# First batch's row fetches in 16 KB pieces, one table for both row parities, wider stand-in matmuls and two moved items

## The chip, the cores and the metric

The kernel runs on one core of a Trainium2 chip. The metric is the device time of one execution in microseconds (us). The engines are named as the profile names them: PE (TensorE, with its weight loads as PEld), DVE (VectorE), ACT (ScalarE), POOL (GpSimd) and SP (SyncE, which here only issues DMAs). All data are fp32.

## The reference

Eight batches of 3008 tokens by 256 channels go through a spectral filter along the token axis, and the result, as one list of 24064 tokens, goes through a two-layer block with SiLU:

```python
def _attn_ref(x, filt_r, filt_i):            # x: 8 x 3008 x 256
    X = np.fft.rfft(x, axis=1)
    Y = X * (filt_r + 1j * filt_i)[None, :, :]
    return np.fft.irfft(Y, n=x.shape[1], axis=1)

def _moe_ref(x, w_in, w_out):                # x: 24064 x 256, w_in: 256 x 2048, w_out: 2048 x 256
    h = x @ w_in
    return (h * (1.0 / (1.0 + np.exp(-h)))) @ w_out
```

## The kernel before

The transform of length 3008 is done as small matmuls: 3008 = 94 x 32, so a batch is 94 rows of 32 columns n. Stage 1 transforms along the rows (tiles `pa`, or `pf` in later batches), `forward` along the columns (`pb`), DVE multiplies with the filter, `inverse` goes back along the columns (`pc`), and stage 3 goes back along the rows (`pd`). Its results are copied into `y`, which feeds the two-layer block. [...]

The two-layer block is one long loop of 384 steps, 48 pairs of token groups by 8 slices of the hidden layer. Each step multiplies two slices of `w_in` (lines 1001 and 1047, tiles `px` and `pyz`) and projects the step before (line 1093, tile `acc`). From step 6 on the block products are done with seven matmuls in place of eight, by a Strassen-like scheme; `tokens` (line 978) makes the sums of token blocks that it needs (tile `ty`, three DVE instructions for one pair). The spectral work of the later batches is slipped into the steps at hand-written places: `put(step, round, piece)` appends a piece to `pending`, and `until` writes out what is due. Each engine works its own instructions in the order in which the program writes them.

The first batch comes before the loop and is written out by hand (lines 1338 to 1453). For it `inverse_first` gives, for each of six groups g, tiles `pc` that `rows_first` copies to SBUF and `store_half` (line 700) sends to `d2[0]` (columns 0 to 15) and later to `d2[1]` (columns 16 to 31). `fetch_rows` (line 723) brings `d2[0]` back with the summed axis on the partitions, in three pairs of DMAs on SP's queue, for rows 0 to 15, 16 to 31 and 32 to 47. The element order of a row in `d2` is (n, h, c): column n of 16, row parity h of 2, channel c of 256. A DMA of a pair takes one parity h: 16 rows of 16 pieces of 256 channels (1 KB each), onto partitions of the lower half (h = 0) or the upper half (h = 1) of the tile `us["t4"]`, which lies in the still unused weight tile `w_t`. The third pair waits for the stores of groups 4 and 5, the last of which is issued at line 700 by SP.

Stage 3 of group g (line 730) then multiplies four columns, `t4[rows, i, ...]`, with the table `wi_t` (at this time filled from `ws_tbl`: for each parity the 64 rows of that parity's partitions). `pd_g_0` holds parity 0, from the lower partitions, and `pd_g_1` parity 1. `evict_y` (line 757) copies them into `y`, in four runs of 47. Groups 0 to 3 make columns 0 to 15, that is pairs 0 to 2 of the loop, groups 4 to 7 the other half, with another load (`load_t4`). Groups 0 to 2 come before the loop, group 3 in step 1. For groups 0 to 2 ACT copies `pd_g_0` and DVE `pd_g_1`; for group 3 DVE copies `pd_3_0` and ACT `pd_3_1`.

Before the loop the eight PSUM banks go round by a counter, `early[0]` (line 354): each new tile takes the next of f, f, a0, a1, a2, a3, x, yz. `idle(n, operand, m)` (line 1324) is n matmuls of m columns that compute nothing that is used; it takes a bank of its own and so moves the counter by one. There are two: 26 of 36 columns at the start, before the first data are there (line 1341), and 2 of 96 columns ahead of stage 3 (line 1436).

The chain around that place is, in the order of the program:

```python
    out_of(3, 2, copy=act)
    gp.tensor_copy(out=gate, in_=part["us"]["t4"][:, 0, 0:1])
    ...
    idle(2, m=96)
    early[0] -= 1
    part["stage3"](0)
    out_of(3, 3, copy=act)
    early[0] += 2
    part["stage3"](1)
```

Here `out_of(3, q)` copies the four tiles `pa_3_q` that the second batch's stage 1 (line 425) has made just before; q = 0 and 1 go to DVE, 2 and 3 to ACT.

The second batch's pieces are placed by `plan` (line 827), relative to step 48: `multiply` (line 621) is two DVE instructions of 128x512 that read `pb` and the filter. The tokens of pair 2 are written by lines 1499 to 1501.

Of the kernel before, what the change touches and what calls it, by code (L numbers as in the profile page):

```python
# [46 lines left out]
FP32 = mybir.dt.float32  # L47
# [8 lines left out]
N1, N2 = 47, 64  # L56
# [218 lines left out]
def kernel(  # L275
# [10 lines left out]
    nc = tc.nc  # L286
    ctx.enter_context(tc.manual_schedule())

    wx_host, wq_host, wi_host, d_host, e_host = dft_tables()
# [1 line left out]
    wx3_dram = nc.inline_tensor(np.tile(wx_host.reshape(3, 32, 128).transpose(1, 0, 2), (4, 1, 1)).copy(), name="wx3_tbl")  # L291
    wq_dram = nc.inline_tensor(wq_host, name="wq_tbl")
    wi_dram = nc.inline_tensor(wi_host, name="wi_tbl")
    ws_host = np.zeros_like(wi_host)
    for k, (first, by) in enumerate(SPREAD):
        for h in range(2):
            ws_host[64 * h + first:64 * h + first + 15 * by + 1:by] = wi_host[64 * h + 16 * k:64 * h + 16 * k + 16]
    ws_dram = nc.inline_tensor(ws_host, name="ws_tbl")
    d_dram = nc.inline_tensor(d_host, name="d_tbl")
    e_dram = nc.inline_tensor(e_host, name="e_tbl")  # L300
# [9 lines left out]
    cpool = pool("consts", 1)  # L310
# [18 lines left out]

    wx_t = cpool.tile([96, 128], FP32)  # L330
    wq_t = cpool.tile([128, 4, 32], FP32)
    wi_t = cpool.tile([128, N1], FP32)
    wm_t = cpool.tile([128, 32], FP32)
    d_t = cpool.tile([128, NS, 2, 32], FP32)
    e_t = cpool.tile([128, NG, 2, 2, 64], FP32)
# [16 lines left out]
    y = {}  # L352
# [18 lines left out]
    def spectral(b):  # L371
# [3 lines left out]
        d2 = dpool.tile([2 * NS, 32, 2, C] if b else [2, 2 * NS, 16, 2, C], FP32, name=f"d2_{b}", tag="d2")  # L375
        xs, us, t2s, banks, prods, halves, t4s = {}, {}, {}, {}, {}, {}, {}
# [346 lines left out]
        def fetch_rows(a0, n, *queues):  # L723

            k, r0 = divmod(a0, 16)
            for h in range(2):
                queues[h].dma_start(out=us["t4"][64 * h:64 * h + 64].rearrange("(q r) n c -> q r n c", r=4)[r0:r0 + n, k],
                                in_=d2[0, a0:a0 + n, :, h, :])

        def stage3(g, home=None):  # L730

            half, n0 = divmod(4 * g, 16)
            ps = [bank(b, f"pd_{b}_{g}_{h}", home[h] if home else None)
                  .rearrange("p a c -> p (a c)")[:, 0:8 * N1]
                  .rearrange("p (a i n) -> p a i n", a=2, i=4) for h in range(2)]
            t4 = us["t4"][:, 4 * g:4 * g + 4] if g < 4 else t4s[g]
            for cb in range(2):
                for i in range(4):
                    for c0 in (0, 64):
                        for h in range(2):  # L740
                            rows = slice(64 * h, 64 * h + (64 if g < 4 else 2 * NS))
                            nc.tensor.matmul(  # L742
                                out=ps[h][c0:c0 + 64, cb, i, :],
                                lhsT=t4[rows, i, 2 * c0 + cb:2 * c0 + 128:2],
                                rhs=wi_t[rows, :], start=True, stop=True)
            if 3 < g < 6:
                load_t4(g + 2)
            if n0 == 0:
                y[b, half] = ypool.tile([128, 2, HALF], FP32, name=f"y_{b}_{half}", tag="y")
            if early[0] is None:  # L750
                us["pd", g] = ps
                return
            us["pd", g] = ps
            for h in range(2):
                evict_y(g, h, nc.vector.tensor_copy if h else nc.scalar.copy)

        def evict_y(g, h, copy=None):
            half, n0 = divmod(4 * g, 16)
            dst = y[b, half].rearrange("p a (n h r) -> p a h n r", n=16, h=2)
            copy = copy or (nc.scalar.copy if h else nc.vector.tensor_copy)  # L760
            copy(out=dst[:, :, h, n0:n0 + 4], in_=us["pd", g][h])

        def load_wide(k):
            t4s[k] = [t4pool.tile([128, 8, C // 2], FP32, name=f"t4_{b}_{k}_{cb}", tag="t4") for cb in range(2)]
# [56 lines left out]
    def put(step, rnd, piece, *args):  # L821

        pending.append((step + rnd / ROUNDS, len(pending), lambda: piece(*args)))
# [3 lines left out]
    def plan(b, part):  # L827

        at = STEPS * b

        if b > 1:
            put(at - {2: 80, 3: 120}.get(b, 128), 0, part["reverse_x"])
            early_fold = (-73, ((-68, 3), (-68, 5), (-65, 3), (-64, 3))), (-89, ((-82, 5), (-81, 3), (-81, 5), (-75, 5)))
            for f, step, load, places, ends in (
                    (0, -64, *early_fold[b > 2], ((1, 0), (1, 3))),
                    (1, -56, -63, ((-61, 5), (-60, 3), (-60, 5), (-59, 3)), ((1, 3), (2, 3))),
                    (2, -48, -55, ((-52, 3), (-52, 5), (-51, 5), (-50, 5)), ((1, 3), (2, 3)))):
                put(at + load, 4 if load == -89 else 0, part["load_fold"], f)
                for k, (fold_step, rnd) in enumerate(places):
                    put(at + fold_step, rnd, part["fold"], f, k)  # L840
                put(at + step, 7, part["stage1_fold"], f)
                put(at + step, 7, part["evict_fold"], f)
                for q, (after, rnd) in enumerate(ends):
                    put(at + step + after, rnd, part["pairs_fold"], f, q)
                joined.add(at + step)
                opened.add(at + step + 1)
            put(at - 47, 0, part["load_fold"], 3)
            for k, (step, rnd) in enumerate(((-45, 3), (-45, 5), (-44, 3), (-44, 5))):
                put(at + step, rnd, part["fold"], 3, k)
            early_out.add(at - 43)  # L850
            open_step(at - 43, (part["stage1_fold"], 3), (part["evict_fold"], 3))
            put(at - 43, 3, part["pairs_fold"], 3, 0)
            put(at - 43, 5, part["pairs_fold"], 3, 1)
            return plan_two(b, part)
        put(at - 38, 0, part["load_t2"], 0)
        put(at - 38, 0, part["load_t2"], 1)
        for g, places in enumerate((
                ((-36, 3), (-36, 5), (-35, 3), (-35, 5), (-34, 5)),
                ((-35, 6), (-34, 3), (-33, 3), (-33, 5), (-32, 1)),
                ((-32, 7), (-31, 0), (-31, 2), (-28, 5), (-27, 2)),  # L860
                ((-27, 3), (-27, 5), (-26, 5), (-25, 3), (-24, 3)),
                ((-24, 7), (-23, 0), (-23, 2), (-20, 2), (-20, 5)),
                ((-20, 3), (-19, 3), (-19, 5), (-18, 3), (-18, 5)))):
            pieces = (("forward", g), ("multiply", g, 0), ("multiply", g, 1), ("add", g, 0), ("add", g, 1))
            for (step, rnd), (piece, *args) in zip(places, pieces):
                if piece != "forward" or g in (1, 3, 5):
                    put(at + step, rnd, part[piece], *args)
        open_step(at - 36, *last_part[0](5), (part["forward"], 0))
        for g, step in ((0, -32), (2, -24), (4, -16)):
            put(at + step, 7, part["inverse"], g, 2)  # L870
            if g < 4:
                pending.append((at + step + 7 / ROUNDS, 10 ** 6 + 9, lambda g=g: part["forward"](g + 2, ACCS)))
                joined.add(at + step)
            put(at + step, 7, part["even"], g, 0, 2)
            put(at + step, 7, part["even"], g, 1, 2)
            put(at + step + 1, 5, part["rows"], g, 0, 2)
            put(at + step + 2, 3, part["rows"], g, 1, 2)
        plan_rest(b, part)
# [445 lines left out]
    def idle(n, operand=None, m=128):  # L1324

        ps = bank(0, "idle").rearrange("p a c -> p (a c)")
        rows = (wx_t if operand is None else operand)[:, 0:m]
        for _ in range(n):
            nc.tensor.matmul(out=ps[0:m, 0:m], lhsT=rows, rhs=rows, start=True, stop=True)
# [8 lines left out]
    wide_rows = d_t[0:96].rearrange("p s r n -> p (s r n)")[:, 0:256]  # L1338
    blank = w_t.rearrange("p j c w n -> p (j c w n)")[0:96, 6144:6272]
    v.memset(blank, 0.0)  # L1340
    idle(26, operand=blank, m=36)

    part, second = spectral(0), spectral(1)
    part["load_first"]()
# [5 lines left out]
    nc.sync.dma_start(out=f_all[:, :, 4:], in_=filt_b)  # L1350
    nc.sync.dma_start(out=d_t[:, 16:NS], in_=d_dram[:, 16:NS])
    nc.sync.dma_start(out=e_t[:, 2:NG], in_=e_dram[:, 2:NG])
    nc.sync.dma_start(out=wi_t, in_=ws_dram.ap())
    weights(0, 1)
    second["load_pair"](1)
    second["load_pair"](2)
# [76 lines left out]
            for i in range(2):  # L1433
                part["store_half"](g, i, 1, gp)
    halves_of(2, 3)
    idle(2, m=96)
    early[0] -= 1
    part["stage3"](0)
    out_of(3, 3, copy=act)
# [53 lines left out]
    per = len(PAIRS) * 2  # L1493


    combines = ((-2, 1), (6, 1), (11, 5), (22, 1), (26, 6), (38, 1))
    stores = (((10, 1), (10, 5)), ((19, 1), (23, 5)), ((31, 1), (31, 5)), ((35, 1), (35, 5)),
              ((43, 1), (43, 5)), ((50, 1), (51, 1)))
    for pair in range(len(pairs)):
        step, rnd = combines[pair % per] if pair > 2 else ((5, 2), (11, 1), (12, 1))[pair]  # L1500
        pending.append((pair // per * STEPS + step + rnd / ROUNDS, 98, lambda pair=pair: tokens(pair)))
        for chunk in range(2 if pair < len(pairs) - 1 else 0):
            step, rnd = stores[pair % per][chunk] if pair else (14, 1 + 4 * chunk)
            pending.append((pair // per * STEPS + step + rnd / ROUNDS, 99 + chunk,
                            lambda pair=pair, chunk=chunk: output(pair, chunk)))
# [65 lines left out]
```

## Time and profile before

| | |
|---|---|
| median of 3 executions | 2485.16 us (2485.12 to 2485.7) |
| the profiled execution | 2485.27 us |
| its span, first to last instruction | 2483.1 us |
| around the span | 2.2 us |
| PE busy | 2472.1 us, 16272 matmul records |
| DVE, ACT, POOL busy | 1748.4, 1087.1, 438.9 us |
| granted TensorE clock, mean | 1.000 |
| DMA | 170.68 MB, mean 69 GB/s |

The profile is of one execution. Its groups of instructions give busy time, mean duration and the idle time of the engine ahead of them, with what ended it. The timeline lists instructions in order of time, merged where they follow each other. The chain of waits follows the last instruction back through whatever released each step. One fp32 matmul of the program shows as two matmul records and two weight loads. Positions such as 48.8 us are counted from the start of the span.

### The profile page before, as it was taken

The numbers are of one execution on the slowest core, as the hardware profiler recorded it, in microseconds if no ns is written. First come the engines' busy times: TensorE is split into PE (matmuls) and PEld (weight loads), VectorE is DVE, ScalarE is ACT, GpSimd is POOL, SyncE is SP. The second block draws the span as 40 slices with busy tenths as digits, with TensorE's granted clock in tenths as the row PEclk, the third lists the DMA queues.
The fourth block names the chain that finished last, engine by engine and source line by source line (L and its number), as shares of the span: only waits on it lengthen the run. The fifth ranks groups of instructions, "written<-read, shape, count | busy, mean of one in ns | idle before, by whom it ended". The sixth has DMA issues, their size and how long they took to land.

```text
span 2483.1 us, 42315 instructions
## 1 busy us (share of the span) xinstructions
PE 2472.1 (100%) x16272; PEld 2124.9 (86%) x16272; DVE 1748.4 (70%) x3577; ACT 1087.1 (44%) x2986; POOL 438.9 (18%) x683
## 2 busy tenths in 40 slices
PE   9999999999999999999999999999999999999999
PEld 6888888888888888888888888889888888888988
DVE  7876777777777777786777767777777767655544
ACT  4534444444444444444444444444444444444443
POOL 4121112112221112211221112211221121101100
PEclk9999999999999999999999999999999999999999
DMA  8432225203242033320333114221142211200000
GB/s 327 148 98 77 74 63 117 63 14 93 61 109 61 25 78 81 96 54 26 88 83 89 49 29 108 60 69 43 51 98 47 56 51 32 59 22 9 17 10 17
DMA packets 139881, 170.68 MB, mean 69 GB/s; under 512 B 20972, under 2 KB 113484, under 8 KB 139148
## 3 DMA queue, kind: packets, MB, share of 16 engines
q1 hardware_dynamic: 116416, 121.74, 18.4%
q0 software_dynamic: 22272, 44.89, 6.9%
q8 instruction: 128, 2.10, 0.4%
q10 hardware_dynamic: 992, 1.36, 0.2%
q14 instruction: 73, 0.60, 0.1%
HBM read 96.06 MB, written 81.26 MB: 71 GB/s over the span
## 4 chain that ended last, share of the span: by engine, by line
PE 99%; DVE 0%; DMA 0%; POOL 0%; ACT 0%; issue 0%; SPq 0%; DVEq 0%
PE acc L1093 46%; PE px L1001 26%; PE pyz L1001 19%; PE pd L779 1%; PE pf L504 1%; PE pc L598 1%; PE pb L560 1%; PE pa L401 1%; PE pc L676 0%; PE px L1047 0%; PE pyz L1047 0%; PE pb L542 0%; PE pd L742 0%; PE pc L656 0%; DMA d<-w_t 0%; DMA w_t<-d 0%
## 5 line engine op out<-in xcount | busy, mean ns | idle before, releaser
L1093 PE MATMUL acc<-g,w_t 128*128 128x256 f32 (+1 forms) x5388 | 1513.1, 376 | 3.0 <-ACT o L792 2.5
L1093 PEld LDWEIGHTS acc<-g,w_t 128*128 128x128 f32 x5388 | 1019.8, 190 | 153.1 <-ACT o L792 15.3
L972 DVE TENSOR_TENSOR g<-pyz,abc 128x256 f32<-128x256 f32 (+1 forms) x1134 | 472.3, 416 | 468.2 <-ACT abc L1022 228.4
L972 DVE TENSOR_TENSOR g<-g 128x512 f32<-128x512 f32 (+1 forms) x1134 | 581.3, 513 | 193.8 <-ACT g L1005 180.8
L1001 PE MATMUL px<-ty,w_t 128*128 128x256 f32 (+1 forms) x2268 | 665.5, 375 | 0.0
L1005 ACT ACTIVATE g<-g 128x256 f32<-128x256 f32 (+1 forms) x1134 | 465.4, 410 | 231.9 <-DVE g L972 231.9
L972 POOL TENSOR_TENSOR s<-s 128x256 f32<-128x256 f32 (+1 forms) x331 | 254.3, 785 | 1436.4 <-DVE s L1121 981.8
L1001 PEld LDWEIGHTS px<-ty,w_t 128*128 128x128 f32 x2268 | 427.9, 190 | 52.1 <-issue 0.8
L1001 PE MATMUL pyz<-y,w_t 128*128 128x256 f32 (+1 forms) x1512 | 444.0, 375 | 1.1 <-DVE g L972 1.1
L1001 PEld LDWEIGHTS pyz<-y,w_t 128*128 128x128 f32 x1512 | 279.4, 189 | 42.3 <-DVE g L972 2.9
L1016 ACT COPY abc<-px 128x256 f32<-128x256 f32 (+1 forms) x378 | 139.1, 368 | 366.6 <-PE px L1001 366.6
L1005 ACT ACTIVATE g<-px 128x256 f32<-128x256 f32 (+1 forms) x378 | 143.5, 380 | 298.1 <-PE px L1001 298.0
L1022 ACT COPY abc<-px 128x256 f32<-128x256 f32 (+1 forms) x378 | 139.2, 368 | 307.3 <-PE px L1001 307.2
L1001 PE MATMUL px<-y,w_t 128*128 128x256 f32 (+1 forms) x756 | 223.5, 377 | 0.0
L1001 PE MATMUL pyz<-ty,w_t 128*128 128x256 f32 (+1 forms) x756 | 222.1, 376 | 0.0
L1001 PEld LDWEIGHTS px<-y,w_t 128*128 128x128 f32 x756 | 141.7, 189 | 21.1 <-DVE q L800 1.9
L1001 PEld LDWEIGHTS pyz<-ty,w_t 128*128 128x128 f32 x756 | 139.9, 190 | 20.2 <-DVE g L972 0.4
L1009 ACT COPY abc<-px 128x256 f32<-128x256 f32 (+1 forms) x378 | 133.0, 352 | 34.5 <-PE px L1001 34.5
L524 POOL DMA_DIRECT2D d<-tf x96 | 48.5, 505 | 212.9 <-DVE tf L454 212.9
L1121 ACT COPY s<-acc 128x512 f32<-128x512 f32 (+2 forms) x99 | 56.1, 566 | 49.0 <-issue 28.5
L619 POOL DMA_DIRECT2D d<-low x36 | 22.3, 618 | 292.5 <-DVE low L615 279.0
L494 DVE TENSOR_TENSOR uf<-x_all 120x512 f32<-120x512 f32 (+1 forms) x72 | 60.2, 864 | 0.3 <-issue 0.3
(134 smaller groups left out, 1390.2 us busy)
## 6 DMA issues: line engine op xcount, KB each, us to landing
t<-d SPq DMA_DIRECT2D x84, 256.0 KB
t<-d SPq DMA_DIRECT2D x224, 96.0 KB
out_dram<-s SPq DMA_DIRECT2D x64, 256.0 KB
d<-q POOLq DMA_DIRECT2D x48, 256.0 KB, 5.3
x_all<-in_x_dram SPq DMA_DIRECT2D x96, 96.0 KB
x_all<-xr SPq DMA_DIRECT2D x96, 96.0 KB
d<-tf POOLq DMA_DIRECT2D x96, 96.0 KB, 2.7
d<-tq POOLq DMA_DIRECT2D x96, 96.0 KB, 2.8
```

The costliest lines, as they stand in the source:

```text
L401: nc.tensor.matmul(out=ps[q], lhsT=wx3_t[rows, k], rhs=xs[j][rows, k], start=(k == 0), stop=(k == 2), skip_group_check=True)
L494: nc.vector.tensor_tensor(out=out, in0=in0, in1=in1, op=op)
L504: nc.tensor.matmul(out=ps[q][32 * k:32 * k + 32], lhsT=wq_t[rows, k], rhs=rhs[k][rows], start=True, stop=True)
L524: nc.gpsimd.dma_start(out=d1[par, :, grp, at:at + 4], in_=part[rows].rearrange("p q n c -> p (q n) c"))
L972: eng.tensor_tensor(out=out, in0=in0, in1=in1, op=op)
L1001: nc.tensor.matmul(out=out, lhsT=w_t[:, jp, c, 0], rhs=rhs, start=start, stop=True, skip_group_check=True)
L1005: nc.scalar.activation(out=g[:, k, 0:n], in_=g[:, k, 0:n] if src is None else src, func=AFT.Silu)
L1009: nc.scalar.copy(out=sums[:, 0, 0:n], in_=xo)
L1016: nc.scalar.copy(out=sums[:, 1, 0:n], in_=xo)
L1022: nc.scalar.copy(out=sums[:, 2, 0:n], in_=xo)
L1093: nc.tensor.matmul(out=acc[pair][i][:, h, 0:n], lhsT=w_t[:, jp, OUT_PLACE.get(c, c), 1], rhs=g[:, k, 0:n], start=i not in touched, stop=la ...
L1121: copy(out=dst, in_=src)
```

## The change

- `fetch_rows` splits a row by columns in place of parities: the first DMA of a pair takes columns 0 to 7, the second columns 8 to 15, both parities, so that each row is one run of 4096 elements (16 KB). The lower partitions then hold columns 0 to 7 and the upper ones 8 to 15, with the parities alternating along the free axis.
- The table gets a place for each parity on all partitions: `ws_t` [128, 2, 47] in place of `wi_t` [128, 47]; its load doubles from 188 to 376 bytes per partition. `wi_t` is its first half and is reloaded at step 5 as before.
- Stage 3 of groups 0 to 3 takes the table by `i % 2`, so `pd_g_0` now holds columns 2g and 2g + 1, both parities, and `pd_g_1` columns 8 + 2g and 9 + 2g. `evict_y` writes one run of 188 for these groups in place of four of 47; the layout of `y` is as before.
- The stand-ins at the start are 16 of 58 columns in place of 26 of 36. Those ahead of stage 3 are gone, while `early[0] -= 1` behind them stays.
- `multiply(0, 0)` of the second batch goes from step 12, round 5 to step 12, round 3, and the tokens of pair 2 from step 12, round 1 to step 12, round 0.

The number of PE instructions falls by 12 matmuls; on every other engine the number is the same.

```diff
-    ws_host = np.zeros_like(wi_host)
+    ws_host = np.zeros((2, 64, 2, N1), wi_host.dtype)
     for k, (first, by) in enumerate(SPREAD):
         for h in range(2):
-            ws_host[64 * h + first:64 * h + first + 15 * by + 1:by] = wi_host[64 * h + 16 * k:64 * h + 16 * k + 16]
+            ws_host[:, first:first + 15 * by + 1:by, h] = wi_host[64 * h + 16 * k:64 * h + 16 * k + 16]
+    ws_host = ws_host.reshape(128, 2 * N1)
...
-    wi_t = cpool.tile([128, N1], FP32)
+    ws_t = cpool.tile([128, 2, N1], FP32)
+    wi_t = ws_t[:, 0]
...
-                queues[h].dma_start(out=us["t4"][64 * h:64 * h + 64].rearrange("(q r) n c -> q r n c", r=4)[r0:r0 + n, k],
-                                in_=d2[0, a0:a0 + n, :, h, :])
+                queues[h].dma_start(out=us["t4"][64 * h:64 * h + 64].rearrange("(q r) n c -> q r (n c)", r=4)[r0:r0 + n, k],
+                                in_=d2[0, a0:a0 + n, 8 * h:8 * h + 8].rearrange("a n h c -> a (n h c)"))
...
-                                rhs=wi_t[rows, :], start=True, stop=True)
+                                rhs=ws_t[rows, i % 2 if g < 4 else 0], start=True, stop=True)
...
-            dst = y[b, half].rearrange("p a (n h r) -> p a h n r", n=16, h=2)
             copy = copy or (nc.scalar.copy if h else nc.vector.tensor_copy)
-            copy(out=dst[:, :, h, n0:n0 + 4], in_=us["pd", g][h])
+            if g < 4:
+                dst = y[b, half].rearrange("p a (k n r) -> p a k n r", k=2, r=N1)[:, :, h, n0:n0 + 4]
+            else:
+                dst = y[b, half].rearrange("p a (n h r) -> p a h n r", n=16, h=2)[:, :, h, n0:n0 + 4]
+            copy(out=dst, in_=us["pd", g][h])
...
-                ((-36, 3), (-36, 5), (-35, 3), (-35, 5), (-34, 5)),
+                ((-36, 3), (-36, 3), (-35, 3), (-35, 5), (-34, 5)),
...
-    idle(26, operand=blank, m=36)
+    idle(16, operand=blank, m=58)
...
-    nc.sync.dma_start(out=wi_t, in_=ws_dram.ap())
+    nc.sync.dma_start(out=ws_t.rearrange("p h n -> p (h n)"), in_=ws_dram.ap())
...
     halves_of(2, 3)
-    idle(2, m=96)
     early[0] -= 1
     part["stage3"](0)
...
-        step, rnd = combines[pair % per] if pair > 2 else ((5, 2), (11, 1), (12, 1))[pair]
+        step, rnd = combines[pair % per] if pair > 2 else ((5, 2), (11, 1), (12, 0))[pair]
```

## Prediction

> **What bounds the kernel.** I read the page first: whether one engine fills the span, and whether the chain that ended last leaves it.
>
> ```profile
> PE 2472.1 (100%) x16272; PEld 2124.9 (86%) x16272; DVE 1748.4 (70%) x3577; ACT 1087.1 (44%) x2986; POOL 438.9 (18%) x683
> ...
> PE 99%; DVE 0%; DMA 0%; POOL 0%; ACT 0%; issue 0%; SPq 0%; DVEq 0%
> ```
>
> PE is idle for 2483.1 - 2472.1 = 11 us in all. A change that leaves the matmuls alone can only win back idle PE time, and 0.2% of the time (5 us, about what a measurement of this kernel can tell from no change) is nearly half of that. So next I read what PE waited for (total, times, longest):
>
> ```profile
> PE acc L1093 <- ACT o L792: 2.5, 3, 0.8
> PE pd L742 <- DMA w_t<-d: 1.4, 2, 0.9
> PE pyz L1001 <- DVE g L972: 1.1, 1, 1.1
> ```
>
> The first row lies in later batches, out of reach of the diff. The second is stage 3 waiting for the row fetches, the third lies at 141 us, in step 13. The rest of the span is matmul behind matmul, so what is won at these two places stays won. PE's timeline at the first place (start, length):
>
> ```profile
> 47.68 0.58 PE L1329 MATMUL idle<-wx_t 96*96 96x96 f32 x4
> 48.82 0.29 PE L742 MATMUL pd<-wi_t,w_t 64*64 64x47 f32 x2 [0.56 <-DMA w_t<-d]
> 49.99 3.09 PE L742 MATMUL pd<-wi_t,w_t 64*64 64x47 f32 x190 [0.89 <-DMA w_t<-d]
> 53.01 1.13 PE L1047 MATMUL px<-y,w_t 128*128 128x256 f32 x4
> ```
>
> Useful work ends at 47.75 (line 425's last matmul) and goes on in earnest at 49.99: 2.24 us, of which the stand-ins fill 0.58. The chain of waits tells why:
>
> ```profile
> 40.22 4.83 DMA d<-w_t
> ...
> 45.75 4.11 DMA w_t<-d
> 49.99 3.09 PE pd L742 x190
> ```
>
> The last store of group 5 is issued at 40.22 and lands at 45.05; only then SP issues the third fetch pair, whose second half lands at 49.86.
>
> **The fetches.** Bytes, number of DMAs and queue stay; the pieces change from 1 KB to 16 KB. By the trace's packet records a 1 KB packet takes 46 ns at the median, one of 8 KB 314 ns, one of 32 KB 1213 ns. Half of the last is 607 ns for 16 KB, against 16 x 46 = 736 ns, or some 850 ns at the 50 to 55 ns that crowded 1 KB packets take. All 16 engines work on a fetch (one row each), so a pair takes 1.2 us in place of 1.5 to 1.7: 0.3 to 0.5 us less. This counts twice: the first pair (issued at 37.76) lies ahead of the last stores in SP's queue, and the third is awaited itself. The other bound is the only packets of just this size, PE's instruction pages on the queue of kind "instruction": 1095 ns, by which a pair takes 2.2 us, 0.5 to 0.7 more. [...]
>
> The store has more to lose. By its semaphore records 15 of its 16 parts were confirmed by 43.64 and the last at 45.05; the stores beside it show the same straggler (43.27, then 44.57; 43.45, then 44.79). At 42.03 an instruction page of PE begins that takes 1.44 us. Stores with nothing in the way took 2.0 to 2.7 us (37.21 to 39.18, 35.48 to 38.20). The change takes 10 matmuls, 40 records, out ahead of this point, so the page falls due 40 records later, about 2.3 us at the pace of line 425 (144 records in 8.4 us), near 44.3. The store then lands at 43.6 or sooner. The page now meets the third pair; it can cost the engine it sits on up to 1.1 us.
>
> ```profile
> 41.16 5.19 SPq L727 DMA_DIRECT2D w_t<-d  x4
> 46.40 1.54 SPq L1208 DMA_DIRECT2D raw<-in_moe_w_dram  x3
> ```
>
> The row of 5.19 holds two pairs and SP's wait for the store between them. SP issued the third pair at 45.19 and 45.75, and it landed 3.4 and 4.1 us later (48.57, 49.86). Issued at 43.7 and 44.3 it lands by 47.1 and 48.4 with nothing else gained, some 0.5 us sooner with the larger pieces. What SP has queued behind (weights, then line 447's stores) moves up with it, by about as much as PE, so the weights arrive no later relative to their use; the nearest, raw 3, lands at 53.27 for a use at 54.52.
>
> **The removed stand-ins.** They cost nothing where PE waits anyway. But `early[0] -= 1` stays, so the banks shift by one: `pd_0_0` moves from a0 to the first f, which holds `pa_3_2` until ACT has copied it. The instruction order shows the new wait: on ACT in place of PE. ACT's row for that copy starts at 47.78 and takes 0.58, so stage 3 cannot start before 48.36 + 0.1 = 48.46. Behind the waiting matmul the whole PE queue waits. This, and not the fetch, is late next. `pd_1_1` goes to bank x (free at 48.0, DVE) and `px` waits for its copy by DVE, which ends near 51.1; `pyz` of step 0 now needs `pd_2_0`'s copy by ACT, which ends near 52.0, for a start at 52.4. Both fit, with 0.4 us to spare. Step 2 now needs `pd_3_0`, copied by DVE from 62.21 to 62.76; its first matmul came at 64.78.
>
> So stage 3 starts at 48.46 in place of 49.99: **-1.5 us**. Cover gone (ACT or the page late by 1 us): -0.5.
>
> **The copies into y and the table.** Four copies on ACT of 478 ns, four on DVE of 550 ns, in longer runs: I take no change; one copy's 0.5 us is the bound either way, since only the last one of ACT is near the path. The table's load is 24 KB more at 13 us, for a use at 48 us: nothing.
>
> **The stand-ins at the start.** 52 records took 3.34 us from 1.08. With 58 columns, 32 records take between 32 x 60 ns = 1.9 (if the pace does not go by width) and 32 x 97 ns = 3.1 us (if it does). The first real matmul waits for a load that lands at 4.17. Nothing, if PE reaches full speed as before: line 401's groups come 0.85 us apart until 7.92 and 0.43 from 8.55 on. One group more at the slow pace costs 0.4 us, and an earlier switch gives at most 0.3, as the loads end that.
>
> **The two moved items.** DVE around step 12:
>
> ```profile
> 134.80 0.42 DVE L972 TENSOR_TENSOR g<-pyz,abc 128x256 f32<-128x256 f32 x1 [1.59 <-ACT abc L1009]
> 135.14 0.88 DVE L972 TENSOR_TENSOR g<-g 128x256 f32<-128x256 f32 x2
> 135.94 0.65 DVE L972 TENSOR_TENSOR ty<-y 128x480 f32<-128x480 f32 x1
> 136.62 0.85 DVE L972 TENSOR_TENSOR ty<-y,ty 128x240 f32<-128x240 f32 x2
> ...
> 139.05 0.68 DVE L635 TENSOR_TENSOR z<-pb,filt 128x512 f32<-128x512 f32 x1
> 139.65 0.68 DVE L635 TENSOR_TENSOR p<-pb,filt 128x512 f32<-128x512 f32 x1
> 140.25 0.42 DVE L972 TENSOR_TENSOR s<-acc,s 128x256 f32<-128x256 f32 x1
> 140.58 0.42 DVE L972 TENSOR_TENSOR g<-pyz,abc 128x256 f32<-128x256 f32 x1
> ```
>
> PE's stall at 141.05 is the last row: it frees the bank that step 13 writes. DVE was idle for 1.59 us ahead of 134.80. In the new order the three `ty` instructions (1.45 us) come first and fill that time, with no wait of their own in the program; `z` and `p` (1.20 us) take their place at 135.94. The next sum still waits for ACT's copy (136.94 + 0.38), so it and the four copies of `acc` keep their times up to 139.05; then come the `s` row and the last sum, at 139.38. No DMA is moved. PE could go on at 139.71 and now does at 139.87: **-1.2 us** (bounds 0 to -1.34).
>
> **Sum**, against the profiled execution's 2485.27 (0.1 over the median): -1.5 - 1.2 = -2.7, **2482.6 us**.
>
> **Rivals.** (a) *Fetches no sooner.* The straggler stays, or the page holds up the third pair: stage 3 starts near 49.9, and only step 12 gains: 2484.1. For it: the store's landing hangs on one page's place. [...] (b) *Step 12's stall stays or moves on*, because another wait ends last there: 2483.8. Against it: each predecessor's row is above. (c) *Slower: too few DMA engines take the 16 pieces.* The copy at line 460, 46 rows of 32 KB, ran two packets at a time for 28 us. On two engines a half takes 8 x 0.607 = 4.9 us, six halves 29, and stage 3 starts near 69: +18, 2503. On four it is near 54.8, 2489; from five engines up the kernel is still faster. Against it: the present fetch has the same 16 rows outermost, and 16 engines confirm it; line 460 has 2 outermost. [...]
>
> **Chances.** Forecast 0.6, (a) 0.2, (b) 0.1, (c) 0.05, the rest 0.05 either way. The range of 8 in 10 takes in (a) and (b), and below the forecast the early switch and step 12's bound: 2481.7 to 2484.7. Faster by over 0.2% 0.03, within 0.92, slower 0.05, by the stalls' sizes and (c).
>
> **What would show it.** 16 KB packets near 610 ns on SP's queue; the last store landing near 43.5; stage 3 starting near 48.5 behind ACT's copy of `pa`; no wait of PE for DVE near 139.9. Wrong if the fetch lands after 48.4, if `px` or `pyz` of steps 0 to 2 shows a wait, or if a wait for weights turns up in the first steps.

## The result, and the profile after

The changed kernel takes 2490.57 us (median of 22 executions, 2484.34 to 2492.88), the kernel before 2486.16 us (22 executions beside them, 2484.57 to 2487.77): a ratio of 1.0017, 95% interval 1.001 to 1.0023. The forecast was 2482.6 us, in a range up to 2484.7; the change made the kernel some 4.4 us slower, not 2.7 us faster. The profiled execution took 2490.95 us with a span of 2488.5 us, 5.4 more than before.

PE's busy time hardly changed, so the page's first lines tell little (before: 2472.1 us of 2483.1):

```profile
PE 2474.1 (99%) x16248; PEld 2124.1 (85%) x16248; DVE 1749.3 (70%) x3577; ACT 1088.7 (44%) x2986; POOL 439.0 (18%) x683
```

What PE waited for, in the changed kernel (total, times, longest):

```profile
PE pd L744 <- issue: 3.7, 1, 3.7
PE acc L1098 <- ACT o L797: 2.5, 3, 0.8
PE pc L678 <- issue: 1.2, 1, 1.2
PE idle L1334 <- DVE w_t L1345: 1.1, 1, 1.1
PE pd L744 <- ACT w_t L444: 0.7, 1, 0.7
```

(Line numbers have moved: 425 is now 427, 676 is 678, 742 is 744, 1047 is 1052.) Both rows that the prediction set out to remove are gone: no wait for DVE in step 13, and at stage 3 a wait for ACT's copy in place of the fetches, as forecast. In their place stand two rows released by "issue", time in which the engine waited for nothing that the profile shows. PE's timeline places the large one in the middle of stage 3 (start, length, idle time ahead):

```profile
49.41 2.01 PE L744 MATMUL pd<-ws_t,w_t 64*64 64x47 f32 x115 [0.67 <-ACT w_t L444]
55.08 2.37 PE L744 MATMUL pd<-ws_t,w_t 64*64 64x47 f32 x77 [3.67 <-issue]
57.38 2.07 PE L1052 MATMUL px<-y,w_t 128*128 128x256 f32 x4
59.25 1.91 PE L1052 MATMUL pyz<-y,w_t 128*128 128x256 f32 x4
60.96 1.36 PE L1052 MATMUL px<-y,w_t 128*128 128x256 f32 x4
62.16 1.03 PE L1052 MATMUL pyz<-y,w_t 128*128 128x256 f32 x4
```

Before, stage 3's burst was one row of 3.09 us, and the `px` and `pyz` groups behind it took 1.13 and 1.03 us. So there are two losses: 3.67 us of nothing, and then matmuls at nearly twice their length. The windows of the changed kernel say what the second is (us, busy times, then the granted clock PEclk, DMA share, GB/s):

```profile
48.00:51.40 3.40, 2.73 (x121) 1.95 (x116) 2.09 (x4) 1.58 (x4) 3.12 (x6) 1.00 0.87 271
51.40:55.10 3.70, 0.04 (x6) 0.02 (x3) 0.00 (x0) 0.27 (x1) 2.88 (x6) 0.96 0.97 334
55.10:61.60 6.50, 6.50 (x87) 5.60 (x87) 5.10 (x10) 1.73 (x5) 4.09 (x9) 0.50 0.84 274
61.60:68.00 6.40, 6.40 (x64) 5.42 (x66) 2.77 (x5) 3.96 (x8) 4.10 (x9) 1.00 0.84 292
```

The granted clock is 0.50 until 61.6. The trace's clock record has it from 54.80 for 6.83 us, twice 3.41, and 54.80 lies 14 times 3.41 us behind the moment at which full clock began (7.01). In the 3.41 us just ahead of it (51.39 to 54.80) PE was idle for 3.38 us. Less was enough elsewhere: with the old start stand-ins put back (the first experiment below) half clock also followed 3.41 us with 1.39 us of idle PE (47.79 to 51.20), while in the run with two weight loads moved it did not follow 3.41 us with 1.63 us of idle PE (50.13 to 53.54). So the runs show no amount of idle time at which the clock falls.

What "issue" stands for is seen by counting. I counted PE's records (matmuls, weight loads and semaphore waits) from the start of the program. PE stopped behind record 961 (the 1.15 us at 35.44, line 678) and behind record 1473, 512 later. The queue of kind "instruction" with 127 packets of 16 KB fits PE: its 16248 matmuls and as many weight loads, 32496 records, are 256 for each packet.

```profile
q8 instruction: 127, 2.08, 0.3%
```

So I take both stops to be at page boundaries, two pages apart, a page being one such packet. A page is named here by the record at its boundary, reckoned in steps of 256 from the two stops. When each page's packet started, from the packet records, with the PE record that was then running:

```
                         page for record 961   page for 1217     page for 1473      page for 1729
before                   30.50 (at 810)        34.98 (999)       42.03 (1188)       54.94 (1696)
changed                  34.10 (926)           38.68 (1040)      52.68 (1473)       58.56 (1634)
```

In the changed kernel the page that holds stage 3's second half starts at 52.68, 1.26 us after PE ran dry at 51.42, takes 1.03 us, and PE goes on 1.37 us after its end. Before, it had landed (43.47) nearly 8 us ahead of use. The 40 records of the ten start stand-ins are missing ahead of it (the eight records of the other two stand-ins lie behind line 425, too late to move record 1217). Three theories stood at this point: **1, the count of PE records** (the 48 that went) makes the page late; **2, the 16 KB fetch pieces** crowd it out; **3, the stand-ins ahead of stage 3** are needed for the clock.

### The profile page after: what moved, and what is told of

Its sections match the earlier page's. It is cut to its first block, busy times and chain, and to the rows that moved or that the text cites. A ratio compares the mean times of both kernels' runs of the same rounds, so it can differ in the third digit from the quotient of the medians.

```text
span 2488.5 us, 42266 instructions
## 1 busy us (share of the span) xinstructions
PE 2474.1 (99%) x16248; PEld 2124.1 (85%) x16248; DVE 1749.3 (70%) x3577; ACT 1088.7 (44%) x2986; POOL 439.0 (18%) x683
## 4 chain that ended last, share of the span: by engine, by line
PE 99%; DMA 0%; issue 0%; ACT 0%; POOL 0%; DVE 0%; SPq 0%; DVEq 0%
PE acc L1098 46%; PE px L1006 26%; PE pyz L1006 19%; PE pd L784 1%; PE pf L506 1%; PE pc L600 1%; PE pb L562 1%; PE pc L678 0%; PE px L1052 0%; PE pyz L1052 0%; PE pa L427 0%; PE pb L544 0%; PE pd L744 0%; PE pa L403 0%; DMA w_t<-in_x_first_dram 0%; PE pc L658 0%
```

## The experiments

Ratios are to the kernel before on the same chip, with 95% intervals.

**One part at a time.** The start stand-ins put back, in the changed kernel:

```
-    idle(16, operand=blank, m=58)
+    idle(26, operand=blank, m=36)
```

> The changed kernel with the start stand-ins as before (26 of 36 columns instead of 16 of 58; 40 PE records more ahead of everything). Theory 1, instruction supply: the boundary at which PE ran dry (record 1473 of PE and PEld) falls back 40 records in the work and its page is asked for in time; no stall for want of instructions near 51 us, full clock throughout, 2482.0 to 2483.0 us. Theory 2, the 16 KB fetch pieces crowd out PE's instruction page: the stall of 3.7 us and the half clock stay, 2490 us. Theory 3, the removed stand-ins ahead of stage 3 are what the clock needs: the half clock stays, 2487 to 2490 us.

Measured: 2484.39 us, 0.9991 (0.9982 to 1.0); no row released by "issue", the page for record 1473 at 42.97.

The reverse edit in the kernel before (1 KB pieces, stand-ins ahead of stage 3 in place):

> The kernel before with the start stand-ins alone changed (16 of 58 columns). Theory 1: PE runs dry near record 1473 although the fetches are of 1 KB pieces and the stand-ins ahead of stage 3 are there; one stall for want of instructions of 1 to 4 us, with or without a stretch of half clock behind it, 2486 to 2493 us. Theories 2 and 3: no stall, 2484.5 to 2486 us.

Measured: 2492.05 us, 1.0018 (1.001 to 1.0027). PE's waits:

```profile
PE pd L742 <- issue: 3.9, 1, 3.9
PE acc L1093 <- ACT o L792: 2.5, 3, 0.8
PE pc L676 <- issue: 1.2, 1, 1.2
PE pyz L1001 <- DVE g L972: 1.1, 1, 1.1
```

Both stops are there, at records 961 and 1473, with no 16 KB piece in the kernel and the old stand-ins ahead of stage 3. So the edit of the start stand-ins alone brings the whole loss; the second and third theories fall as its cause.

The two moved items alone, in the kernel before:

> The kernel before with the two moved items alone. All theories: no wait of PE for DVE near 141 us, 1.2 us sooner than before (2484.0 to 2484.9 beside about 2485.6). If the changed kernel's loss lay in the moved items, slower than before.

Measured: 2485.25 us, 0.9993 (0.9984 to 1.0002). The interval holds 1.0; the trace shows the wait for DVE gone:

```profile
139.97 0.59 PE L1001 MATMUL pyz<-y,w_t 128*128 128x256 f32 x2
140.40 0.59 PE L1001 MATMUL px<-y,w_t 128*128 128x256 f32 x2
140.83 0.64 PE L1093 MATMUL acc<-g,w_t 128*128 128x256 f32 x2
141.36 0.70 PE L1001 MATMUL pyz<-y,w_t 128*128 128x256 f32 x2
```

The fetches by columns and the table alone:

> The kernel before with the fetches by columns and the table for both parities alone (all stand-ins and items as before). Theory 1: no stall for want of instructions; stage 3 starts up to 1 us sooner, 2484.3 to 2486 us. Theory 2: the stall of some 3.7 us near 51 us and half clock behind it, 2489 to 2492 us.

Measured: 2485.92 us, 0.9997 (0.9989 to 1.0006), no stop by "issue". Stage 3 still waited for its fetches from `d2`, which lies in DRAM (before: 1.4, 2, 0.9):

```profile
PE pd L744 <- DMA w_t<-d: 1.7, 2, 1.1
```

**Records, or the length of the stand-ins?** Ten stand-ins of 4 columns behind the 16 of 58 bring the 40 records back:

```
     idle(16, operand=blank, m=58)
+    idle(10, operand=blank, m=4)
+    early[0] -= 1
```

> The changed kernel with ten more stand-ins of 4 columns behind the 16 of 58 (the 40 PE records back, but not the old width). Theory 1, the place of the instruction page counts: no stall for want of instructions near 51 us, a page packet near 43 us as in the kernel before, 2483.5 to 2485.5 us. Rival: the width and length of the start stand-ins (when full clock begins) set it: the stall of 3.7 us stays, 2489 to 2492 us.

Measured: 2484.77 us, 0.9991 (0.9982 to 1.0), the page at 42.48, no stop. So it is the records that matter, and not the columns. (Stage 1 starts later in this run, at 5.16 us in place of 4.46. The runs further down that put eight records at 311 or later leave the start as it was.)

**Does the page wait in line behind the weight loads?** SP's three weight loads (issued at 45.76 to 46.85) moved behind four later stores, and then only two of them:

```
     part["fetch_rows"](32, 16, nc.sync, nc.sync)
-    weights(3, 4, 5)
...
-    bits(3)
-    added(3)
     for u in (6, 7):
         second["store_rows"](u, nc.sync)
+        weights(*((3, 4, 5) if u == 6 else ()))
+    bits(3)
+    added(3)
     weights(6)
```

> The changed kernel with SP's three weight loads (issued from 45.76 us on) moved behind four of SP's later stores, near 51.5 us; ACT's and DVE's work on the third slice moves with them. Theory 1 in its finer form, the page request waits in line on its DMA engine behind what was issued before it: with the weight loads gone from ahead of it the page starts between 46 and 50 us and not at 52.7, and the stall of 3.7 us at record 1473 shrinks under 1 us. Rival: the page is not asked for before PE reaches its end (a demand fetch): it starts 1.3 us after PE stops, and the stall stays at 3 to 4 us. The time says little here, since the third slice comes 5 us late: 2484 to 2492 us by either.

> As the run before, but only the second and third of the weight loads moved behind SP's four stores. Waiting in line: the page waits for one load instead of up to three and starts between 49 and 51.8 us; the stall falls from 3.7 to 0 to 2.8 us; 2483.5 to 2489 us. Demand fetch: the stall stays at 3 to 4 us and the time at 2489 to 2492 us.

Measured: 2488.35 us, 1.0007 (0.9998 to 1.0016), and 2487.58 us, 1.0003 (0.9994 to 1.0012). The stop at record 1473 is 3.67, then 2.29 (two loads moved), then 2.02 us (three), and the page starts at 52.68, 51.99 and 51.22. So what stood ahead of the page makes up 1.4 to 1.7 us of the stop, and no more. With all three loads moved both theories missed: the page came neither before 50 nor after PE had run dry (it started 0.9 us before PE reached 1473). With two moved, the stop and the time lay where waiting in line had them, and the page came 0.2 us later than that. The windows of the run with all three loads moved, of the same columns as above:

```profile
48.00:49.00 1.00, 1.00 (x14) 0.42 (x6) 0.96 (x2) 0.97 (x2) 0.92 (x2) 1.00 0.01 0
49.00:50.00 1.00, 0.45 (x6) 0.00 (x0) 0.91 (x2) 0.54 (x2) 0.92 (x2) 1.00 0.00 0
50.00:51.00 1.00, 0.88 (x55) 0.89 (x55) 0.38 (x1) 0.06 (x1) 0.90 (x3) 1.00 0.00 0
51.00:52.00 1.00, 1.00 (x76) 1.00 (x69) 0.54 (x1) 0.58 (x2) 1.00 (x3) 1.00 0.80 172
```

The DMA engines stood empty from 48 to 51 us (share 0.01, 0.00, 0.00) and the page did not start. The profile has no record of a request; the likeliest reading is that the page had not been asked for, so that the request itself is late. It started 1.1 us after PE's sequencer passed the last semaphore wait ahead of stage 3 (50.11).

**Is it that wait, standing on the page, that holds the request back?** More start stand-ins of 58 columns in steps of two (`idle(18, ...)` to `idle(24, ...)`):

> The changed kernel with 18 start stand-ins of 58 columns in place of 16 (8 PE records more; stage 3's semaphore waits stand 8 records later on the instruction page that begins at record 1217). Theory A, a semaphore wait of PE ahead of stage 3 holds back the request for the page of record 1473: the page starts over 1 us after stage 3's data are there, near 51 to 53 us, and the stall of 2 to 4 us stays; 2488 to 2492 us. Theory B, only the queues decide, the earlier the boundary the sooner the page: it starts some 0.5 us sooner than 52.7, the stall is near 3 us.

> As before with 20 (16 records more). A: all or nothing, a page either before 46 us with no stall, or after 50.5 with 2 to 4 us of it; from the kernel before with 16 stand-ins, where the wait stands 12 records later than in the changed kernel and the page was late, it should still be late. B: page near 51.5, stall near 2.5 us.

> As before with 22 (24 records more). A: all or nothing again; if the page is early here, it lies between SP's last store and its weight loads (43.5 to 46 us), the store has no straggler, the third fetch pair goes out near 44.6 as in the changed kernel, and the time is the best of all, 2482.5 to 2484 us. B: page near 50.5, stall near 1.5 us.

> As before with 24 (32 records more). A: page before 46 us, no stall for want of instructions, 2483 to 2485 us. B: page near 49.5, stall under 1 us.

```
start stand-ins   page for 1473 starts   stop at 961   stop at 1473   us        ratio (95%)
16 (changed)      52.68                  1.15          3.67           2490.57   1.0017 (1.001 to 1.0023)
18                46.43                  1.16          none           2485.45   0.9995 (0.9985 to 1.0004)
20                47.03                  1.57          none           2485.59   0.9996 (0.9986 to 1.0005)
22                44.49                  none          none           2483.99   0.9988 (0.9978 to 0.9997)
24                43.77                  none          none           2484.60   0.9993 (0.9983 to 1.0002)
```

All or nothing, as the theory of the held request (A) has it, but already with 18, where A had expected the stall to stay: eight records decide over 3.67 us. Theory B, by which the page comes a little sooner with each step, falls: it had a stall near 3 us with 18. A was then put to a sharper test: the same eight records just ahead of line 425's last group (48 records long), so that the wait stands at the same place as with 18 but nothing earlier moves.

```
     out_of(1, 3, copy=dve)
+    idle(2, m=4)
+    early[0] -= 1
     second["stage1_pair"](3)
```

> The changed kernel, start stand-ins as changed, with two stand-ins of 4 columns (8 PE records) just ahead of line 425's last group. Nothing before 40 us differs from the changed kernel, so the first stall for want of instructions (1.2 us at 35.4) stays. If what decides is where stage 3's semaphore wait stands on the instruction page: the page starts near 46 us, no stall of 3.7 us, hardly a run at half clock, 2485 to 2486.5 us, as with 18 start stand-ins. If it is the start of the kernel (length of the stand-ins, start of full clock, the first page): as the changed kernel, 2489 to 2492 us.

Measured: 2491.08 us, 1.0013 (1.0004 to 1.0022), the page at 53.88:

```profile
49.18 1.99 PE L744 MATMUL pd<-ws_t,w_t 64*64 64x47 f32 x111 [0.74 <-ACT w_t L444]
56.13 2.48 PE L744 MATMUL pd<-ws_t,w_t 64*64 64x47 f32 x81 [4.96 <-issue]
58.54 2.07 PE L1052 MATMUL px<-y,w_t 128*128 128x256 f32 x4
```

Theory A in that form falls. But two of these ten executions took 2484.70 and 2485.54 us at a mean clock of 1.000, as two of the 22 of the changed kernel did (2484.34 and 2486.90). None of the four was profiled; by their times they had no loss, or only part of it, so the place of the records does not decide alone. Three more places for the same eight records, ahead of the first `forward` group (record 311), of the third `inverse` group (832), and of line 425's second group (1093):

> The changed kernel with two stand-ins of 4 columns (8 PE records) just ahead of the first group of forward (record 311 or so), in place of at the start. If the start of the kernel decides (length of the stand-ins): as the changed kernel, 2489 to 2492 us, page near 52 us. If it is only how many records stand ahead of the boundaries: as with 18 start stand-ins, page near 46.5 us, no stall of 3.7 us, 2485 to 2486 us.

> The changed kernel with the same 8 records ahead of the third inverse group (record 832 or so), between the boundaries at 705 and 961. If the cut of the page that begins at 961 or after decides: page near 46.5 us, no stall of 3.7 us, 2485 to 2486 us. If an earlier page's cut decides: as the changed kernel, 2489 to 2492 us.

> The changed kernel with the same 8 records ahead of the second batch's second stage-1 group (record 1093 or so), between the boundaries at 961 and 1217. If the cut at 1217 decides: page near 46.5 us, no stall of 3.7 us, 2485 to 2486 us. If the cut at 961 or an earlier one decides: as the changed kernel, 2489 to 2492 us, as the 8 records at 1189 gave.

Measured: 2485.39 us, 0.9997 (0.9987 to 1.0006); 2484.74, 0.9994 (0.9984 to 1.0003); 2484.69, 0.9995 (0.9986 to 1.0005). In all three the page starts at 46.1 to 46.5 and stage 3 runs through; of the third:

```profile
36.98 0.37 PE L678 MATMUL pc<-w_t,minus 64*64 64x256 f32 x1 [1.17 <-issue]
...
49.79 3.55 PE L744 MATMUL pd<-ws_t,w_t 64*64 64x47 f32 x192 [0.67 <-DMA w_t<-d]
53.27 1.13 PE L1052 MATMUL px<-y,w_t 128*128 128x256 f32 x4
54.24 1.03 PE L1052 MATMUL pyz<-y,w_t 128*128 128x256 f32 x4
55.10 1.03 PE L1052 MATMUL px<-y,w_t 128*128 128x256 f32 x4
```

So neither the start of the kernel nor the cuts of the pages that begin at 705 and 961 decide; eight records anywhere up to 1093 do, at 1189 they don't. What the five kernels with a late page have in common is a semaphore wait of PE at about record 1189, 28 ahead of the boundary at 1217 (in the changed kernel it is the wait of line 425's last group; with the eight records at 1189 it is their own, and the group's follows at 1198). The kernels with 16 to 24 stand-ins and the page in time have that group's wait at 1197 or later, those with 26 at about 1229, and none at 1189. That fits all profiled executions, but it is a pattern found afterwards, not a mechanism shown: three of the five (the changed kernel and the two with moved loads) have the same PE instructions, and the changed kernel itself also once ran in 2484.34 us.

**Is more of the gap ahead of stage 3 to be filled?** The old start stand-ins, and two stand-ins ahead of stage 3 in a bank of their own:

```
-    idle(16, operand=blank, m=58)
+    idle(26, operand=blank, m=36)
...
+    idle(2, m=96)
-    early[0] -= 1
+    early[0] -= 2
```

> The changed kernel with the old start stand-ins (26 of 36) and with the two stand-ins of 96 columns back ahead of stage 3, in a bank of their own so that stage 3 keeps the changed kernel's banks. The gap ahead of stage 3 goes from 0.8 to about 0.2 us. Theory of the clock, a window of 3.4 us with too much idle PE is followed by one at half clock: fewer runs at 0.999 than 4 in 11, median 2483.5 to 2484.4 us. Rival, the gap before stage 3 has nothing to do with the half clock: as a_stand26, 2484.4 us, a third of the runs at 0.999.

Measured: 2485.43 us, over both forecasts, 0.9992 (0.9983 to 1.0001), 4 of 11 executions with a mean clock under 1.000, as without them (4 of 11): no effect seen. The gaps stayed at 0.9 and 0.6 us, as the fetches landed later in this execution, so the clock theory was not really tried; it is an assumption from the clock records above.

**Are the larger pieces worth anything?** The best kernel above (22 stand-ins) with 1 KB pieces:

> The kernel before with 22 start stand-ins of 58 columns, without those ahead of stage 3, and with the two moved items: the best kernel so far but for its 1 KB fetch pieces. If larger pieces shorten the fetches by the 0.3 to 0.5 us a pair that was forecast: stage 3 starts some 0.5 us later than with 22 stand-ins and 16 KB, 2484.5 us. If they are worth nothing: the same 2484.0 us.

Measured: 2484.62 us, 0.9992 (0.9984 to 1.0001), beside 0.9988 (0.9978 to 0.9997) with 16 KB pieces. By time they can't be told apart. In the traces stage 3's long row starts 0.47 us later with 1 KB pieces (50.30 and 49.83), but line 425's first wait already came 0.53 us later (38.42 and 37.89), and the last store took 3.71 us in place of 4.37, the second half of the third pair 4.87 in place of 4.29. One execution of each settles nothing.

## Why the prediction was wrong

**The step that failed** is the sentence on PE's instruction page: "the page falls due 40 records later, about 2.3 us at the pace of line 425 (144 records in 8.4 us), near 44.3", with "it can cost the engine it sits on up to 1.1 us" as its only price. I treated the page as one more DMA that takes time from a fetch, and its arrival as a given. By the count it is PE's own next 256 instructions (32496 records in 127 packets); it started not 2.3 but 10.7 us later, and PE stopped for 3.67 us in stage 3's burst (115 matmuls in the 2.01 us ahead of the stop). I had counted the 40 records and looked at what the page does to others, not at what waits for it. In the changed kernel PE's waits show two stops by "issue" for 127 pages, of 1.15 and 3.67 us.

**The sum, term by term**, on the profiled executions. Forecast span 2483.1 - 2.7 = 2480.4, measured 2488.5, so 8.1 us are to be found. Stage 3 began 0.95 us later than forecast: the stop at 961 put 1.15 us ahead of it, less 0.2. From there to the third `px` row (63.02, at full clock) it took 13.61 us; in the run with eight records ahead of record 1093 it took 7.04 (49.79 to 56.83). The difference is 6.57 us, of which 3.67 are the stop, and the other 2.9 the half clock. The remaining 0.46 is the burst itself, 3.48 us to the first `px` row in that run (49.79 to 53.27) in place of 3.02 before (49.99 to 53.01). That makes 8.0 of the 8.1.

**Stage 3's start: right in mechanism.** Forecast 48.46 behind ACT's copy of `pa_3_2`. Measured 49.41 behind just this copy, which ran from 48.77:

```profile
48.77 0.59 ACT L444 COPY w_t<-pa 128x512 f32<-128x512 f32 x1 [0.46 <-PE pa L427]
```

Without the 1.15 us at 961 that is 48.26. The last store did lose its straggler: it was issued at 41.21 and landed at 44.47, 3.26 us in place of 4.83, and the third pair went out at 44.61. That a page can make the straggler fits nearly all traces: where the page starts between 42.0 and 43.8, in seven kernels, the last store takes 4.4 to 5.1 us (with 26 stand-ins in the changed kernel it again lands only at 45.73, and the third pair goes out at 45.87); in the eleven where it starts after 45 it takes 3.3 to 3.8. In five of those eleven the price was the late page; in the others the page came behind the store and still in time. 22 stand-ins don't fit: there the page starts at 44.49, but the last part of the store, confirmed at 44.74, is 1.22 us behind the others (43.52), so something else held it. The third pair goes out at 44.88, and stage 3 has this:

```profile
48.60 0.29 PE L744 MATMUL pd<-ws_t,w_t 64*64 64x47 f32 x2 [0.70 <-ACT w_t L444]
49.83 3.09 PE L744 MATMUL pd<-ws_t,w_t 64*64 64x47 f32 x190 [0.94 <-DMA w_t<-d]
52.85 1.13 PE L1052 MATMUL px<-y,w_t 128*128 128x256 f32 x4
```

52.85 in place of 53.01: 0.16 us of the 1.5 forecast. So rival (a), fetches no sooner, is what the change does in this run, the best one, once the page is in time.

**The 16 KB pieces: mis-sized.** Forecast 607 ns each; median 902 ns in the changed kernel, 970 in the run of this part alone. The fastest did take 608 ns, but only 5 of the 96 stayed under 650: I had given the 1 KB pieces their price in a crowd and the 16 KB pieces the price of packets with little beside them. The median is near the 1095 ns that I named as the other bound (the pages), and about as much as 16 pieces of 1 KB at their mean of 58 ns (927 ns). A fetch took 3.96 us from issue to landing on the mean of the six in the changed kernel, 4.11 before; over all profiled kernels 4.05 (fifteen with 16 KB pieces) and 4.27 (four with 1 KB), so some 0.2 us less in place of 0.3 to 0.5. Per engine that is 18.2 GB/s with pieces of 16 KB (902 ns) and 17.7 with 1 KB (58 ns). The 607 ns, scaled from the 32 KB packets of another transfer (1213 ns), were my estimate, and that they and not the pages' 1095 ns would hold for the fetch was shown by no trace.

**The moved items: right.** Forecast -1.2 us. The order on DVE came as forecast (the three `ty` rows ahead, no wait for DVE near 140), in the changed kernel as in the run of this part alone; by time the part is worth 0.9993 (0.9984 to 1.0002), that is 1.7 us less, with an interval from 4.0 less to 0.5 more. Among the executions with a mean clock of 1.000 alone the medians are 2484.61 (7 executions) and 2485.56 (11 of the kernel before), 0.95 less.

**Start stand-ins at nothing: wrong**, by the records that they carry and not by their length. Their 32 records took 3.45 us, over the upper bound of 3.1, yet PE began useful work at 4.46, only 0.11 later than before. **Copies, table and banks:** no cost seen; no wait on a copy of stage 3 turned up in steps 0 to 2. **The slower rival** (too few DMA engines) did not happen: all six fetches were confirmed by 16 engines.

**What stays open** is why the page for record 1473 starts late. That it is asked for late, and not held up on its way, is my reading of the empty DMA engines (share 0.01, 0.00, 0.00 from 48 to 51 us in the run with three loads moved), and no record shows a request; that a wait 28 records ahead of the boundary does it is only argued, and it can't be all, since the changed kernel also once ran without the loss (2484.34 us). Nor is it known why the page for record 961 was late (34.10 in place of 30.50) in every kernel with 16 to 20 stand-ins of 58 columns but the one with ten narrow ones behind them (32.46).

## What to carry to other kernels

An edit that adds or removes a few instructions ahead of a dense burst on PE can turn an instruction page late, as the loss of 40 records of the start stand-ins did here (52.68 in place of 42.03): find one stop by "issue", count the PE records up to it, and mark every 256th from there, as many as a page held here (961, 1217, 1473; the marks are not multiples of 256). No run gives a rule for which place is safe: the burst crosses a mark in every kernel here, and eight records more, at 1093 or before, turned a late page into one in time (52.68 and 46.1 to 46.5). So try a few counts and look at when the page's packet starts. When PE waits for "issue" in a place that has no data to wait for, look at the instruction queue's packets first. And the stop of 3.67 us cost nearly as much again (2.9 us) through the clock, so a small change can lose more than all of the time that it touches; the cure costs little: with 22 start stand-ins in place of 16 stage 1's first part ends 0.13 us later (17.28 and 17.15), and the same change is 0.9988 (0.9978 to 0.9997) of the kernel before. That is the best of all runs, picked afterwards, and its interval overlaps those of several others.

## What the runs showed of the hardware

- In the changed kernel PE stopped by "issue" twice, at records 961 and 1473, for 1.15 and 3.67 us; its instruction queue moved 127 pages. The packets of these two pages took 1.1 and 1.0 us, and PE went on 1.4 us after their ends; at the second, the packet started 1.3 us after PE's stop.
- Eight PE records more in the changed kernel took some 5 to 6 us off the median of 2490.57: 2485.45 with two stand-ins more at the start, 2485.39, 2484.74 and 2484.69 with two matmuls of 4 columns at records 311, 832 and 1093. At record 1189 they did not (2491.08).
- In five profiled kernels a stretch of half clock of 3.41 or 6.83 us came in the first 62 us, behind 3.41 us in which PE was idle for 1.39 us or more; in the run with two loads moved 3.41 us with 1.63 us of idle PE had none behind them. A mean clock under 1.000 was seen in 20 of 22 executions of the changed kernel. Where the profile shows no stop at record 1473 it was seen in 3 of 92 of the kernels with start stand-ins of 58 columns, in 16 of 44 of those with 26 of 36 columns, and in 77 of 143 of the kernel before (five sets), where it goes with some 1.5 to 1.9 us (in the first set medians of 2485.56 and 2487.49). So the wider stand-ins may be worth something on the median after all. Why was not tried.
- A 16 KB piece into one partition takes 0.90 to 1.01 us among other transfers (medians of fifteen kernels), about as long as sixteen of 1 KB (0.93 us at their mean of 58 ns).
